# Attention values multiplied as float32, two heads in the two column halves of the array

## The chip, the cores and the metric

The kernel runs on one core of one Trainium2 chip. The metric is the device time of one execution in microseconds (us), taken as the median of the runs shown. Of the core's engines five matter here: TensorE (PE, with its weight loads shown apart as PEld), VectorE (DVE), ScalarE (ACT), GpSimd (POOL) and SyncE (SP), which issues the transfers.

## The reference, cut to what matters

The kernel computes attention and then two dense layers. The first is a mixture of eight experts whose gate is balanced by eight rounds of row and column sums, the second a layer with a squared ReLU. The change lies in the attention part, in its last product.

```python
def _attn_ref(q, k, v):                 # (4, 8, 576, 64) each: batch, heads, positions, width
    scores = scale * np.matmul(q, k.transpose(0, 1, 3, 2))
    scores = np.where(block_i >= block_j, scores, -1000000000.0)   # blocks of 64 positions
    scores = scores - np.max(scores, axis=-1, keepdims=True)
    attn = np.exp(scores)
    attn = attn / (np.sum(attn, axis=-1, keepdims=True) + 1e-09)
    return np.matmul(attn, v)           # <- the product that is changed

def _moe_ref(x, w_gate, w1, w2):        # x: 2304 x 512, eight experts of width 1024
    ...                                 # P: balanced gate
    for e in range(E):
        out += P[:, e:e + 1] * (np.maximum(x @ w1[e], 0.0) @ w2[e])

def _moe2_ref(x, w_in, w_out):          # width 2048
    r = np.maximum(x @ w_in, 0.0)
    return (r * r) @ w_out
```

## The kernel before, in words

**Pairs and steps.** The 32 heads are taken as 16 pairs. A pair has nine query blocks of 64 positions; block b sees 64(b+1) keys. The rows of both heads lie side by side in the 128 partitions, so one matmul gives the scores of one block for both heads. A pair takes R = 6 steps, and step i works on the blocks of `ROUNDS[i]`. The main loop runs over step numbers r, and in each it calls the events of `ORDER` in turn; each event serves an older step than the one before it, so several steps of a pair, and two pairs, are under way at once. The order of `ORDER` is the order in which the instructions stand on every engine.

**The events.** `S` makes the scores (tile `sc`, L547, float32). `soft` takes the maxima and applies the reciprocal sums (DVE, and POOL for the blocks of `POOL_NORM`, L592). `exp` is ACT's exponential (L579). `T` turns blocks of probabilities with 128-wide transposes into PSUM (L617). `hi` copies the turned blocks on ACT into float32r tiles (`evac_hi`, L639), and `lo` subtracts that copy from the turned block on DVE into a second float32r tile (`evac_lo`, L643). The tiles are `ptx` (group 0, from steps 0 to 2) and `pty` (group 1, from steps 3 to 5), each twice, for the high and the low part.

**The values.** `load_v` brings the values of a pair (320 KB) into tile `v`. `conv_v` splits them in the same way into one tile `vt`: the high part by DVE (L536), the low part by POOL (L537). There is one `v` and one `vt`.

**The product.** `pv(n, g, a)` (L655 to L669) makes for group g and head a the product from three float32r matmuls a part: high by high, low values by high, high by low. Group 0 has parts of 384, 256 and 128 columns, group 1 four of 192 and one of 64, so 9 and 15 matmuls. Each writes PSUM partitions 0 to 63. `PVT = (8, 9, 11, 12)` places the four calls of a pair at its steps 8, 9, 11 and 12. One step later `pv_copy` (ACT, L674) brings the result into `xs`, head a in partitions 64a to 64a+63, and after the last of them `xout` (SP, L679) sends `xs` on.

**The other work.** Once eight pairs are through and the inputs of the first third of the tokens have been split and summed (`form`, on ACT, POOL and DVE, L240 among them), `do_fill` adds work of the expert layer to each step: products `m` (L305 to L307, six float32r matmuls of 384 columns) and outputs `y` (L367 to L369, six of 512 columns), some 1.05 us of PE by the planner's own cost a step. The pieces are counted by step, not by time. What the attention loop has not done of them follows right behind it, and then the rest of the two layers, in one list in a fixed order. The loads at the start stand in the order in which the code issues them: the first pair's k and q, `v`, the identity, the gate's weights, three blocks of expert weights, and then the second pair's k and q (L523).

Of the kernel before, what the change touches and what calls it, by code (L numbers as in the profile page):

```python
# [8 lines left out]
F32 = mybir.dt.float32  # L9
F32R = mybir.dt.float32r  # L10
I32 = mybir.dt.int32
I64 = mybir.dt.int64
ACTF = mybir.ActivationFunctionType
ALU = mybir.AluOpType
# [16 lines left out]
PAIRS = NB * NH // 2  # L31
SCALE = 0.125
R = 6
# [21 lines left out]

POFF = {7: 0, 3: 2496, 6: 512, 5: 2752, 8: 1024, 0: 1600, 2: 1728, 4: 1984, 1: 2368}

ORDER = ["soft", "pvc", "load", "hi", "exp", "S", "fill", "pv", "lo", "T"]

POOL_NORM = (1, 4, 6, 8)  # L60

VSTEP = 7

LAG = 3

PVT = (8, 9, 11, 12)

PVD = 1

# [26 lines left out]
def fused_kernel(ctx: ExitStack, tc: tile.TileContext, q, k, v, wg, w1, w2, u1, u2, ident, out):  # L96
    nc = tc.nc
# [365 lines left out]
    for S in range(len(stages) + 1):  # L463
        a = products(S) if S < len(stages) else []
        b = outputs(S - 1) if S else []
        if a:
            piece(lambda S=S: begin(S))
        for z in WEAVE:
            src = a if z == "m" else b
# [28 lines left out]
    def attention():  # L498
        with ExitStack() as es:
            at = es.enter_context(tc.tile_pool(name="at", bufs=1))  # L500
            st = es.enter_context(tc.tile_pool(name="st", bufs=4))
            qkv = es.enter_context(tc.tile_pool(name="qkv", bufs=2))
            vp = es.enter_context(tc.tile_pool(name="vp", bufs=1))
            psa = es.enter_context(tc.tile_pool(name="psa", bufs=1, space=PSUM))
            ps = extra["ps"] = es.enter_context(tc.tile_pool(name="ps", bufs=4, space=PSUM))
            vt = at.tile([128, 5, 2, 128], F32R, name="vt")

            pt_x = [at.tile([128, 14, 128], F32R, name=f"ptx{z}") for z in range(2)]
            pt_y = [at.tile([128, 13, 128], F32R, name=f"pty{z}") for z in range(2)]
            scs = [psa.tile([128, w], F32, name=f"sc{z}") for z, w in enumerate((512, 512, 1024))]  # L510
            pb = at.tile([128, 3136], F32, name="pb")
            xs = at.tile([128, 9, 64], F32, name="xs")
            raws = {}
            stat = {}
            tps = {}
            pvs = {}
# [12 lines left out]
            def load_v(n):  # L529
                t = raws["v", n] = vp.tile([128, 640], F32, tag="v", name="v")  # L530
                nc.sync.dma_start(out=t, in_=v[n])

            def conv_v(n):
                t = raws.pop(("v", n)).rearrange("p (j a d) -> p j a d", a=2, d=64)
                hi = vt[:, :, :, 0:64]
                nc.vector.tensor_copy(out=hi, in_=t)  # L536
                nc.gpsimd.tensor_tensor(out=vt[:, :, :, 64:128], in0=t, in1=hi.bitcast(F32), op=ALU.subtract)  # L537

            def width(b):
                return 64 * (b + 1)  # L540
# [78 lines left out]
                    tps[5, 1] = ps.tile([128, 512], F32, tag="g", name="T5")  # L619
                    nc.tensor.transpose(tps[5, 1][0:64, 0:128], pblock(8, 4, 64), idn)  # L620

            def evac_places(i):
                tp = tps[i % 2]
                if i == 0:
                    yield tp, [t[:, 1:14:4] for t in pt_x]
                elif i == 1:
                    yield tp.rearrange("p (a b) c -> p a b c", b=2), [
                        t[:, 2:10].rearrange("p (a b) c -> p a b c", b=4)[:, :, 0:2] for t in pt_x
                    ]
                elif i == 2:  # L630
                    yield tp, [t[:, 0:13:4] for t in pt_x]
                else:
                    yield tp, [t[:, i - 3:i + 7:3] for t in pt_y]
                if i == 5:
                    yield tps[5, 1][0:64, 0:128], [t[0:64, 12] for t in pt_y]

            def evac_hi(i):
                for src, dst in evac_places(i):
                    nc.scalar.activation(out=dst[0], in_=src, func=ACTF.Copy)  # L639

            def evac_lo(i):
                for src, dst in evac_places(i):
                    nc.vector.tensor_tensor(out=dst[1], in0=src, in1=dst[0].bitcast(F32), op=ALU.subtract)  # L643

            def place(n):

# [5 lines left out]
                        t, h = divmod(9 * b + i - 2 * GT * g, 2)  # L652
                        yield g, i, num, (slice(t, t + num), kk, h)

            def pv(n, g, a):  # L655
                p = pvs[g, a] = ps.tile([128, 512], F32, tag="g", name="pv")
                ca = slice(64 * a, 64 * a + 64)
                mm = []
                pts = pt_y if g else pt_x
                if g == 0:  # L660
                    parts = [(0, 0, 6, 0), (1, 6, 4, 128), (2, 12, 2, 256)]
                else:
                    parts = [(j, 3 * j, 3, 0) for j in range(4)] + [(4, 12, 1, 128)]
                for j, i0, nbk, o0 in parts:
                    for t, z in ((0, 0), (0, 64), (1, 0)):
                        mm.append((p[0:64, o0:o0 + 64 * nbk], vt[:, j, a, z:z + 64], pts[t][:, i0:i0 + nbk, ca]))
                mm.append(mm.pop(1))
                for z, (o, l, r) in enumerate(mm):
                    nc.tensor.matmul(o, l, r, start=(z == 0), stop=(z == len(mm) - 1))  # L669

            def pv_copy(g, a):
                w, i0 = (192, 6) if g else (384, 0)
                dst = xs.rearrange("p b c -> p (b c)")[64 * a:64 * a + 64, 64 * i0:64 * i0 + w]
                nc.scalar.activation(out=dst, in_=pvs.pop((g, a))[0:64, :w], func=ACTF.Copy)  # L674

            def xout(n):
                for g, z, num, (t, kk, h) in place(n):
# [34 lines left out]
                yield from form(0)  # L712

            load_qk(0)
            load_v(0)

            for t in pt_y:
                nc.gpsimd.memset(t[64:128, 12].bitcast(F32), 0.0)
            for b in (0, 2, 4, 6):
                nc.gpsimd.memset(pb[:, POFF[b] + width(b):POFF[b] + width(b) + 64], 0.0)  # L720
            nc.sync.dma_start(out=idn, in_=ident)
# [18 lines left out]
            def at_step(fn, r):  # L740
                if 0 <= r < total:
                    fn(*divmod(r, R))
# [11 lines left out]
                     divmod(r - LAG, R) if 0 <= r - LAG < total else None)  # L754

            def turn(r):
                return [(n, z // 2, z % 2) for z, o in enumerate(PVT) for n in [(r - o) // R]
                        if (r - o) % R == 0 and 0 <= n < PAIRS]

            def do_pv(r):  # L760
# [1 line left out]
                    pv(*t)  # L762

            def do_pvc(r):
                for n, g, a in turn(r - PVD):
                    pv_copy(g, a)
                    if g == 1 and a == 1:
                        xout(n)
                        if n >= 4:
                            later.append(n)  # L770
                        if n == 7:
                            tasks.append(first_ready())

            def do_loads(r):
                n, i = divmod(r, R)
                if later:
                    logits_part(later.pop())
                if i == 0 and n + 1 < PAIRS:
                    load_qk(n + 1)
                if r >= VSTEP and (r - VSTEP) % R == 0 and (r - VSTEP) // R < PAIRS:  # L780
                    conv_v((r - VSTEP) // R)
                    if (r - VSTEP) // R + 1 < PAIRS:
                        load_v((r - VSTEP) // R + 1)

            events = {
                "S": lambda r: at_step(scores, r),
                "soft": do_soft,
                "exp": lambda r: at_step(expo, r - 1),
                "T": lambda r: at_step(trans, r - LAG - 1),
                "hi": lambda r: at_step(lambda _, j: evac_hi(j), r - LAG - 2),  # L790
                "lo": lambda r: at_step(lambda _, j: evac_lo(j), r - LAG - 2),
                "pv": do_pv, "pvc": do_pvc, "fill": do_fill, "load": do_loads,
            }
            for r in range(total + R + LAG):
                for e in ORDER:
                    events[e](r)
# [130 lines left out]
```

## Time and profile before

| | us |
|---|---|
| median of 3 runs | 2171.06 |
| lowest and highest | 2168.55 and 2171.75 |
| the profiled execution | 2169.18 |
| its span, first to last instruction | 2167.4 |
| mean granted TensorE clock of it, as a share | 0.996 |

The profile shows one execution. A matmul's duration in it is that of one matmul through the pipeline; matmuls behind each other overlap, so a group's time is read from the chain of work, where each stretch counts once. One float32 matmul stands in the trace as two matmul records with a weight load each; a float32r matmul stands as one. The attention part goes from the start to about 282 us, the rest of the span is the two layers.

### The profile page before, as it was taken

The numbers are of one execution on the slowest core, as the hardware profiler recorded it, in microseconds if no ns is written. First come the engines' busy times: TensorE is split into PE (matmuls) and PEld (weight loads), VectorE is DVE, ScalarE is ACT, GpSimd is POOL, SyncE is SP. The second block draws the span as 40 slices with busy tenths as digits, with TensorE's granted clock in tenths as the row PEclk, the third lists the DMA queues.
The fourth block names the chain that finished last, engine by engine and source line by source line (L and its number), as shares of the span: only waits on it lengthen the run. The fifth ranks groups of instructions, "written<-read, shape, count | busy, mean of one in ns | idle before, by whom it ended". The sixth has DMA issues, their size and how long they took to land.

```text
span 2167.4 us, 32907 instructions
## 1 busy us (share of the span) xinstructions
PE 2124.5 (98%) x11091; PEld 1880.0 (87%) x11091; DVE 1654.7 (76%) x3018; ACT 932.0 (43%) x2299; POOL 1601.5 (74%) x1784
## 2 busy tenths in 40 slices
PE   8989999999999999999999999999999999999998
PEld 6878888889888898889889888988888888888887
DVE  7988858778787767777877767777887667878776
ACT  6766643334434343333434353333434343343432
POOL 4356466678888778778888777787887768878874
PEclk9999999999999999999999999999999999999999
DMA  4433222232323332233232332333222222131211
GB/s 148 121 102 98 67 63 67 85 103 83 98 83 98 98 98 96 85 108 95 81 98 83 98 112 73 108 103 99 82 82 74 69 99 86 59 127 59 95 62 49
DMA packets 80713, 194.62 MB, mean 90 GB/s; under 512 B 26144, under 2 KB 27296, under 8 KB 80544
## 3 DMA queue, kind: packets, MB, share of 16 engines
q1 hardware_dynamic: 80544, 192.53, 28.3%
q8 instruction: 87, 1.43, 0.3%
q14 instruction: 82, 0.67, 0.1%
HBM read 169.95 MB, written 20.97 MB: 88 GB/s over the span
## 4 chain that ended last, share of the span: by engine, by line
PE 87%; DVE 9%; ACT 2%; issue 1%; DMA 1%; SPq 0%; POOL 0%; DVEq 0%; ACTq 0%; POOLq 0%
PE y L369 14%; PE y L368 14%; PE y L367 14%; PE m L306 12%; PE m L305 12%; PE m L307 12%; PE sc L547 3%; PE pv L669 3%; DVE c L285 2%; PE T L617 2%; DVE c L311 1%; DVE h L287 1%; ACT h L286 1%; DVE acc L380 1%; DVE mu L311 0%
## 5 line engine op out<-in xcount | busy, mean ns | idle before, releaser
L367 PE MATMUL y<-b,h 128*128 128x512 f32 x1440 | 566.2, 393 | 18.2 <-ACT h L286 17.6
L369 PE MATMUL y<-b,h 128*128 128x512 f32 x1440 | 574.3, 399 | 0.3 <-DVE h L281 0.3
L305 PE MATMUL m<-x,ah 128*128 128x384 f32 x1680 | 568.3, 338 | 2.2 <-DVE pty L643 1.3
L368 PE MATMUL y<-b,h 128*128 128x512 f32 x1440 | 568.7, 395 | 0.0
L306 PE MATMUL m<-x,ah 128*128 128x384 f32 x1680 | 565.8, 337 | 0.0
L307 PE MATMUL m<-x,al 128*128 128x384 f32 x1680 | 562.1, 335 | 0.0
L166 POOL TENSOR_TENSOR al<-sum,ah 128x256 fp32r<-128x256 f32 x480 | 392.1, 831 | 215.6 <-ACT ah L165 199.6
L280 ACT ACTIVATE h<-c 128x384 fp32r<-128x384 f32 x384 | 201.8, 526 | 736.9 <-DVE c L311 736.7
L387 DVE SCALAR_TENSOR_TENSOR acc<-y,prob,acc 128x512 f32<-128x512 f32 x516 | 383.9, 744 | 80.0 <-PE y L369 78.8
L166 POOL TENSOR_TENSOR al<-raww,ah 128x256 fp32r<-128x256 f32 x360 | 296.3, 823 | 186.2 <-ACT ah L165 141.4
L281 DVE SCALAR_TENSOR_TENSOR h<-c,h 128x384 fp32r<-128x384 f32 x384 | 275.2, 717 | 186.9 <-ACT h L280 186.4
L305 PEld LDWEIGHTS m<-x,ah 128*128 128x128 f32 x1680 | 315.9, 188 | 34.5 <-DVE pty L643 1.6
L306 PEld LDWEIGHTS m<-x,ah 128*128 128x128 f32 x1680 | 315.8, 188 | 34.0 <-issue 1.0
L174 POOL TENSOR_TENSOR b<-raww,b 128x512 fp32r<-128x512 f32 x240 | 325.0, 1354 | 16.1 <-ACT b L173 15.5
L369 PEld LDWEIGHTS y<-b,h 128*128 128x128 f32 x1440 | 269.9, 187 | 64.8 <-DVE h L287 5.9
L367 PEld LDWEIGHTS y<-b,h 128*128 128x128 f32 x1440 | 270.7, 188 | 59.8 <-ACT h L286 23.8
L307 PEld LDWEIGHTS m<-x,al 128*128 128x128 f32 x1680 | 315.6, 188 | 0.0
L368 PEld LDWEIGHTS y<-b,h 128*128 128x128 f32 x1440 | 270.2, 188 | 35.1 <-issue 0.8
L165 ACT ACTIVATE ah<-sum 128x256 fp32r<-128x256 f32 x480 | 183.4, 406 | 148.0 <-POOL sum L149 143.5
L149 POOL TENSOR_TENSOR sum<-raww 128x256 f32<-128x256 f32 x240 | 213.3, 889 | 0.0
L311 DVE TENSOR_TENSOR c<-m,u 128x384 f32<-128x384 f32 x240 | 131.9, 550 | 39.8 <-PE m L307 39.4
L173 ACT ACTIVATE b<-raww 128x512 fp32r<-128x512 f32 x240 | 148.6, 620 | 0.0
(93 smaller groups left out, 2456.9 us busy)
## 6 DMA issues: line engine op xcount, KB each, us to landing
raww<-w_t SPq DMA_DIRECT2D x192, 512.0 KB, 3.7
raww<-w1f SPq DMA_DIRECT2D x24, 512.0 KB, 3.3
raww<-w2f SPq DMA_DIRECT2D x24, 512.0 KB, 3.3
q<-q_d SPq DMA_DIRECT2D x15, 576.0 KB, 4.1
raw<-w_in_bits SPq DMA_DIRECT2D x16, 512.0 KB, 5.2
raw<-w_out_bits SPq DMA_DIRECT2D x16, 512.0 KB, 5.0
acc<-xd SPq DMA_DIRECT2D x30, 256.0 KB, 4.3
v<-v_p SPq DMA_DIRECT2D x16, 320.0 KB, 3.0
```

The costliest lines, as they stand in the source:

```text
L149: nc.gpsimd.tensor_tensor(out=t[:, o], in0=x, in1=y, op=op)
L166: nc.gpsimd.tensor_tensor(out=lo, in0=src, in1=hi.bitcast(F32), op=ALU.subtract)
L174: nc.gpsimd.tensor_tensor(out=lo[:, f], in0=src, in1=hi[:, f].bitcast(F32), op=ALU.subtract)
L280: nc.scalar.activation(out=hh, in_=x3, func=ACTF.Relu)
L281: wait.append(lambda: nc.vector.scalar_tensor_tensor(out=hl, in0=x3, scalar=0.0, in1=hh.bitcast(F32), op0=ALU.max, op1=ALU.subtract,))
L305: nc.tensor.matmul(p, ah[:, k2], bh[:, k2], start=(k2 == 0), stop=False)
L306: nc.tensor.matmul(p, ah[:, k2], bl[:, k2], start=False, stop=False)
L307: nc.tensor.matmul(p, al[:, k2], bh[:, k2], start=False, stop=(k2 == 1))
L367: nc.tensor.matmul(p, hh, bh[:, f], start=(f == 0), stop=False)
L368: nc.tensor.matmul(p, hh, bl[:, f], start=False, stop=False)
L369: nc.tensor.matmul(p, hl, bh[:, f], start=False, stop=(f == 1))
L387: nc.vector.scalar_tensor_tensor(out=a, in0=p, scalar=pe, in1=a, op0=ALU.mult, op1=ALU.add)
```

## The change

The products of the probabilities with the values take float32 operands. So neither the probabilities nor the values are split: the event `lo`, `conv_v` and the tile `vt` go, `ptx` and `pty` stand once, and the values are read from tile `v`, of which there are now two. `pv(n, g)` makes both heads of a group in one call: the matmuls of the two heads alternate, head 0 into PSUM partitions 0 to 63, head 1 into 64 to 127 of the same tile. `pv_copy` copies both heads at once. `PVT` places the two calls of a pair at steps 8 and 11. The first `load_v` moves from the start to step 1, so behind the second pair's k and q.

```diff
-ORDER = ["soft", "pvc", "load", "hi", "exp", "S", "fill", "pv", "lo", "T"]
+ORDER = ["soft", "pvc", "load", "hi", "exp", "S", "fill", "pv", "T"]
-VSTEP = 7
+VSTEP = 1
-PVT = (8, 9, 11, 12)
+PVT = (8, 11)
...
-            vp = es.enter_context(tc.tile_pool(name="vp", bufs=1))
+            vp = es.enter_context(tc.tile_pool(name="vp", bufs=2))
...
-            vt = at.tile([128, 5, 2, 128], F32R, name="vt")
-
-            pt_x = [at.tile([128, 14, 128], F32R, name=f"ptx{z}") for z in range(2)]
-            pt_y = [at.tile([128, 13, 128], F32R, name=f"pty{z}") for z in range(2)]
+
+            pt_x = at.tile([128, 14, 128], F32, name="ptx")
+            pt_y = at.tile([128, 13, 128], F32, name="pty")
...
-            def conv_v(n):
-                t = raws.pop(("v", n)).rearrange("p (j a d) -> p j a d", a=2, d=64)
-                hi = vt[:, :, :, 0:64]
-                nc.vector.tensor_copy(out=hi, in_=t)
-                nc.gpsimd.tensor_tensor(out=vt[:, :, :, 64:128], in0=t, in1=hi.bitcast(F32), op=ALU.subtract)
...
+                nc.scalar.activation(out=dst, in_=tp, func=ACTF.Copy)
...
-            def evac_lo(i):
-                for src, dst in evac_places(i):
-                    nc.vector.tensor_tensor(out=dst[1], in0=src, in1=dst[0].bitcast(F32), op=ALU.subtract)
...
-            def pv(n, g, a):
-                p = pvs[g, a] = ps.tile([128, 512], F32, tag="g", name="pv")
-                ca = slice(64 * a, 64 * a + 64)
-                mm = []
-                pts = pt_y if g else pt_x
+            def pv(n, g):
+
+                p = pvs[g] = ps.tile([128, 512], F32, tag="g", name="pv")
+                vn = raws["v", n].rearrange("p (j a d) -> p j a d", a=2, d=64)
+                pt = pt_y if g else pt_x
...
-                for j, i0, nbk, o0 in parts:
-                    for t, z in ((0, 0), (0, 64), (1, 0)):
-                        mm.append((p[0:64, o0:o0 + 64 * nbk], vt[:, j, a, z:z + 64], pts[t][:, i0:i0 + nbk, ca]))
-                mm.append(mm.pop(1))
-                for z, (o, l, r) in enumerate(mm):
-                    nc.tensor.matmul(o, l, r, start=(z == 0), stop=(z == len(mm) - 1))
-
-            def pv_copy(g, a):
+                for z, (j, i0, nbk, o0) in enumerate(parts):
+                    for a in range(2):
+                        ca = slice(64 * a, 64 * a + 64)
+                        nc.tensor.matmul(
+                            p[ca, o0:o0 + 64 * nbk], vn[:, j, a], pt[:, i0:i0 + nbk, ca],
+                            start=(z == 0), stop=(z == len(parts) - 1),
+                        )
+
+            def pv_copy(g):
                 w, i0 = (192, 6) if g else (384, 0)
-                dst = xs.rearrange("p b c -> p (b c)")[64 * a:64 * a + 64, 64 * i0:64 * i0 + w]
-                nc.scalar.activation(out=dst, in_=pvs.pop((g, a))[0:64, :w], func=ACTF.Copy)
+                dst = xs.rearrange("p b c -> p (b c)")[:, 64 * i0:64 * i0 + w]
+                nc.scalar.activation(out=dst, in_=pvs.pop(g)[:, :w], func=ACTF.Copy)
...
             load_qk(0)
-            load_v(0)
...
                 if r >= VSTEP and (r - VSTEP) % R == 0 and (r - VSTEP) // R < PAIRS:
-                    conv_v((r - VSTEP) // R)
-                    if (r - VSTEP) // R + 1 < PAIRS:
-                        load_v((r - VSTEP) // R + 1)
+                    load_v((r - VSTEP) // R)
```

On PE, in the third pair's steps 2 and 3, this stood in a row before: between two lots of scores (`sc`) the nine float32r matmuls of group 0 for one head (`ptx_109` is the high part, `ptx_110` the low one), then the transposes.

```order
L547 MATMUL sc_115<-k,q 128x320
L669 MATMUL pv<-ptx_109,vt 64x384
L669 MATMUL pv<-ptx_110,vt 64x384
L669 MATMUL pv<-ptx_109,vt 64x256 x2
L669 MATMUL pv<-ptx_110,vt 64x256
L669 MATMUL pv<-ptx_109,vt 64x128 x2
L669 MATMUL pv<-ptx_110,vt 64x128
L669 MATMUL pv<-ptx_109,vt 64x384
L617 MATMUL T<-idn,pb 128x128 x4
```

At the same place of the changed kernel stand the six float32 matmuls of both heads; of each two, the first is head 0 and the second head 1.

```order
L540 MATMUL sc_112<-k,q 128x320
L650 MATMUL pv<-ptx,v 64x384 x2
L650 MATMUL pv<-ptx,v 64x256 x2
L650 MATMUL pv<-ptx,v 64x128 x2
L610 MATMUL T<-idn,pb 128x128 x4
L540 MATMUL sc_110<-k,q 128x448
```

Both heads have moved into one place, and the second place of group 0, one step later, is gone; group 1 goes the same way.

On SP, at the start, this stood before (`w_t` are the expert weights, the last two rows the second pair's k and q):

```order
L527 DMA q<-q_d 128x384
L531 DMA v<-v_p 128x640
L721 DMA idn<-ident 128x128
L722 DMA wgt<-w_gate 128x32
L137 DMA raww_138<-w_t 128x1024
L137 DMA raww_140<-w_t 128x1024
L137 DMA raww_142<-w_t 128x1024
L523 DMA k<-k_t 128x576
L523 DMA q<-q_d 128x1152
```

And this stands there now:

```order
L526 DMA q<-q_d 128x384
L703 DMA idn<-ident 128x128
L704 DMA wgt<-w_gate 128x32
L137 DMA raww_132<-w_t 128x1024
L137 DMA raww_134<-w_t 128x1024
L137 DMA raww_136<-w_t 128x1024
L522 DMA k<-k_t 128x576
L522 DMA q<-q_d 128x1152
L530 DMA v<-v_p 128x640
```

The first pair's values have moved behind the second pair's k and q.

## Rows read from the trace of the kernel before

**Rows 1.** The page, busy time, share and instructions of the engines.

```profile
PE 2124.5 (98%) x11091; PEld 1880.0 (87%) x11091; DVE 1654.7 (76%) x3018; ACT 932.0 (43%) x2299; POOL 1601.5 (74%) x1784
```

**Rows 2.** Windows: stretch, length, each engine's busy us, clock, DMA share, GB/s.

```profile
core 0: us, PE busy (x) PEld busy (x) DVE busy (x) ACT busy (x) POOL busy (x), PEclk, DMA share, GB/s
43.93:56.30 12.37, 12.37 (x95) 10.20 (x95) 11.47 (x41) 9.93 (x29) 4.71 (x5) 1.00 0.40 124
...
204.47:223.85 19.38, 19.38 (x136) 16.83 (x135) 14.19 (x47) 13.48 (x38) 6.42 (x8) 1.00 0.26 76
...
420.00:820.00 400.00, 400.00 (x2006) 359.30 (x2006) 302.67 (x483) 160.22 (x379) 322.77 (x359) 1.00 0.30 95
```

**Rows 3.** The chain through one pair: start us, length us, what.

```profile
43.93 0.87 PE sc L547 x4
44.80 1.24 PE pv L669 x15
46.04 0.44 PE T L617 x4
...
48.44 1.14 PE pv L669 x9
...
50.77 1.04 PE pv L669 x9
...
52.36 0.86 PE sc L547 x2
...
54.63 1.24 PE pv L669 x15
```

**Rows 4.** Weight loads to 290 us: line, shape, count | busy us, mean ns | idle.

```profile
L669 PEld LDWEIGHTS pv<-pty,vt 128*64 128x64 f32 x480 | 43.6, 135 | 6.6 <-issue 1.9 <-DVE pty L643 1.1
...
L305 PEld LDWEIGHTS m<-x,ah 128*128 128x128 f32 x52 | 9.8, 188 | 5.9 <-DVE pty L643 1.6 <-DVE acc L380 1.2 <-PE sc L547 1.0
```

**Rows 5.** The other engines' lines that go or shrink, to 290 us.

```profile
L643 DVE TENSOR_TENSOR ptx<-T,ptx 128x512 fp32r<-128x512 f32 x48 | 32.8, 683 | 4.6 <-ACT ptx L639 4.6
L643 DVE TENSOR_TENSOR pty<-T,pty 128x512 fp32r<-128x512 f32 x48 | 32.8, 683 | 3.9 <-ACT pty L639 3.4
...
L537 POOL TENSOR_TENSOR vt<-v,vt 128x640 fp32r<-128x640 f32 x16 | 24.9, 1558 | 34.7 <-DVE vt L536 27.4 <-PE sc L547 4.2 <-PE lp L693 2.6
...
L674 ACT ACTIVATE xs<-pv 64x384 f32<-64x384 f32 x32 | 15.4, 481 | 10.6 <-PE pv L669 7.0 <-DMA xd<-xs 3.2 <-ACT ah L165 0.3
...
L536 DVE CAST vt<-v 128x640 fp32r<-128x640 f32 x16 | 9.2, 578 | 0.0
```

**Rows 6.** The chain at the start, and what it released.

```profile
7.82 8.78 DMA q<-q_d
...
16.74 2.05 PE sc L547 x4
```

**Rows 7.** Windows of the start and of three longer intervals between pairs.

```profile
0.00:20.00 20.00, 11.76 (x38) 8.35 (x39) 8.69 (x35) 7.82 (x22) 3.02 (x13) 0.88 0.69 232
...
30.47:43.93 13.46, 12.68 (x97) 10.37 (x96) 12.80 (x42) 11.18 (x34) 8.75 (x11) 1.00 0.37 116
...
139.46:162.63 23.17, 17.95 (x117) 14.29 (x116) 21.66 (x48) 15.97 (x45) 20.49 (x21) 0.93 0.34 112
162.63:184.59 21.96, 21.27 (x148) 18.69 (x146) 21.07 (x57) 15.68 (x45) 17.27 (x20) 1.00 0.34 98
```

**Rows 8.** The same windows for PE's work on tile m alone, with its count.

```profile
139.46:162.63 23.17, 2.73 (x12) 0.93 0.34 112
162.63:184.59 21.96, 9.66 (x42) 1.00 0.34 98
```

**Rows 9.** The chain late in the attention: a product's matmul, POOL's split, gate logits.

```profile
182.56 0.17 PE m L305
...
270.26 1.57 POOL vt L537
...
282.19 1.20 PE lp L693 x10
```

More of the change, by code (lines that the diff above doesn't have):

```diff
@@ L620, in trans, with evac @@
                     nc.tensor.transpose(tps[5, 1][0:64, 0:128], pblock(8, 4, 64), idn)
-            def evac_places(i):
+            def evac(i):
                 tp = tps[i % 2]
[L624 to L631, printed above, removed]
-                else:
-                    yield tp, [t[:, i - 3:i + 7:3] for t in pt_y]
+                if i == 1:
+                    dst = pt_x[:, 2:10].rearrange("p (a b) c -> p a b c", b=4)[:, :, 0:2]
+                    tp = tp.rearrange("p (a b) c -> p a b c", b=2)
+                elif i < 3:
+                    dst = pt_x[:, 1 - i // 2:14 - i // 2:4]
+                else:
+                    dst = pt_y[:, i - 3:i + 7:3]
+                nc.scalar.activation(out=dst, in_=tp, func=ACTF.Copy)
                 if i == 5:
-                    yield tps[5, 1][0:64, 0:128], [t[0:64, 12] for t in pt_y]
-            def evac_hi(i):
-                for src, dst in evac_places(i):
-                    nc.scalar.activation(out=dst[0], in_=src, func=ACTF.Copy)
-            def evac_lo(i):
-                for src, dst in evac_places(i):
-                    nc.vector.tensor_tensor(out=dst[1], in0=src, in1=dst[0].bitcast(F32), op=ALU.subtract)
+                    nc.scalar.activation(out=pt_y[0:64, 12], in_=tps[5, 1][0:64, 0:128], func=ACTF.Copy)
             def place(n):
@@ L714, in attention @@
             load_qk(0)
-            load_v(0)
-            for t in pt_y:
-                nc.gpsimd.memset(t[64:128, 12].bitcast(F32), 0.0)
+            nc.gpsimd.memset(pt_y[64:128, 12], 0.0)
             for b in (0, 2, 4, 6):
@@ L756, in turn @@
             def turn(r):
-                return [(n, z // 2, z % 2) for z, o in enumerate(PVT) for n in [(r - o) // R]
+                return [(n, z) for z, o in enumerate(PVT) for n in [(r - o) // R]
                         if (r - o) % R == 0 and 0 <= n < PAIRS]
@@ L764, in do_pvc @@
             def do_pvc(r):
-                for n, g, a in turn(r - PVD):
-                    pv_copy(g, a)
-                    if g == 1 and a == 1:
+                for n, g in turn(r - PVD):
+                    pv_copy(g)
+                    if g == 1:
                         xout(n)
@@ L789, in attention @@
                 "T": lambda r: at_step(trans, r - LAG - 1),
-                "hi": lambda r: at_step(lambda _, j: evac_hi(j), r - LAG - 2),
-                "lo": lambda r: at_step(lambda _, j: evac_lo(j), r - LAG - 2),
+                "hi": lambda r: at_step(lambda _, j: evac(j), r - LAG - 2),
                 "pv": do_pv, "pvc": do_pvc, "fill": do_fill, "load": do_loads,
```

## The prediction, as it was put on record

> **What bounds the kernel now.** I read the page first: PE is busy 98% of the span, no other engine over 76% [rows 1]. A busy PE in this view is not yet a full one, so the next view is the chain of waits in order of time, and there the reader is to see that through a whole pair every piece is PE's, one behind the other [rows 3]. A pair's interval there is 12.37 us, and DVE is busy 11.47 and ACT 9.93 of it [rows 2]. So PE sets the pace and DVE is close behind. In the later intervals the planner's pieces are added on PE (19.38 us an interval, PE busy throughout, DVE 14.19) and the two layers after the attention are PE's from end to end [rows 2]. The pieces are counted by step and the list is fixed, so work that the attention saves moves the end of the attention and with it the end of the kernel, one to one. The change touches nothing behind that.
>
> Three stretches of the attention are not PE's. At the start PE waits for the second pair's q, which takes 8.78 us to land while the expert weights come in as well [rows 6]. The third pair's interval is 13.46 us against 12.37 [rows 2, 7]. And while the first expert inputs are formed, two intervals take 23.17 and 21.96 us, with DVE busy 21.66 and 21.07 of them [rows 7].
>
> **PE's products.** Before, a pair costs 1.24 twice for group 1 and 1.14 and 1.04 for group 0 [rows 3], 4.66 us in all, 24 x 2 matmuls of float32r. Each head has 768 columns in group 0 and 832 in group 1.
>
> A float32 column's price is in the scores: the lot of 512 columns takes 0.86 us [rows 3], 1.68 ns a column. In group 0 three float32r columns cost 1.04/768 = 1.35 ns. So for one head alone float32 is dearer: 1600 x 1.68 = 2.69 us a head, 5.38 us for both if they go one behind the other. That is the upper end, 0.72 us a pair more than now. The lower end is both heads wholly beside each other, 2.69 us, 1.97 less than now.
>
> The trace of before has no place where matmuls of different column halves follow each other (every product sits in partitions 0 to 63, and the scores use all columns), so no row shows which end holds. I take the side by side end, less its lead. What speaks for it: the operands name separate halves of the columns, separate weights, separate output partitions, and the weight loads show that the kernel's products are laid on half the columns (128*64 in [rows 4]). The starts keep the program's order, and a head's own two passes of a part can't overlap. So the pass order is high of head 0, low of head 0 beside high of head 1, low of head 1 beside the next part's high of head 0, and so on: one pass of the first part stands alone. In group 0 that is 768 x 1.68 = 1.29 and a lead of 384 x 0.84 = 0.32, in group 1 832 x 1.68 = 1.40 and 192 x 0.84 = 0.16. Together 3.17 us, and with 0.1 us more, by which the two equal products of group 0 already differ (1.14 and 1.04 [rows 3]), 3.27. Gain 4.66 - 3.27 = 1.39 us a pair, 16 pairs: **22.2 us**. The ends are 31.5 gained and 11.5 lost.
>
> [...]
>
> **Weight loads.** There were 48 a pair and are 32 (16 float32 matmuls, two each). In group 1 each of the 15 matmuls takes 1.24/15 = 83 ns [rows 3], though its weight load lasts 135 [rows 4]: the loads run under the matmuls before them. I cost them at nothing; the cover is the matmul in flight. If it went, one load would show between 53 ns (188 less 135, the price of 64 more columns [rows 4]) and its whole 135 ns: 32 x 16 of them, 27 to 69 us.
>
> **The other engines.** DVE loses six subtractions of about 0.683 us and a cast of 0.578 a pair [rows 5], 4.7 us or more; of 11.47 some 6.8 us stay. POOL loses 1.56 us a pair. ACT loses half of its copies of `pv`, 0.48 us of group 0 and less of group 1 [rows 5]; its 9.93 become some 9.1 us. A pair's interval in the plain part is forecast at 12.37 - 1.39 = 11.0, so all three stay under PE; ACT, the new second, is the closest. A float32 copy on ACT costs what the float32r one did (same elements). The last product of a pair stands at step 11 instead of 12, so `xs` is sent on a step earlier; its copies wait for PE anyway.
>
> **The start.** The first values, 320 KB, no longer stand ahead of the second pair's q. At the 232 GB/s of the first 20 us [rows 7] that is 0.328 MB / 232 = 1.4 us, and PE waits for exactly that transfer [rows 6]. Gain **1.4 us** (0 to 1.5). The values land behind q instead; they are wanted seven steps later. Later loads of values stand behind a pair's k and q on SP, which wait there for the scores of the pair before the last; the values are needed seven steps after that, and with two tiles `v` the load waits for a product two steps back. PE's products now wait for that transfer directly, with the pair's later scores queued behind; I cost it at nothing for those seven steps.
>
> **Stalls that lose their cause.** What the long intervals hold beyond PE's work: the third pair's 13.46 - 12.37 = 1.1. The first long one has the pair's 12.37, 12 matmuls of `m` [rows 8] at 0.173 (0.17 in [rows 9]) = 2.1, and gate logits of 1.2 [rows 9], so 15.7 of 23.17: 7.5 us of stall. The second has 42 matmuls, 7.3, and the same rest, 20.9 of 21.96: 1.1. In the last pairs PE waits for POOL's split of the values, 1.57 us on the chain [rows 9]. DVE loses some 5 us in each long interval. But in the first POOL is busy 20.49 us [rows 7] and loses only 1.56, so that interval can't fall below some 19 us: of 4.2 us at most, 1.4 is the product's gain, and I take 2.5. With 0.8, 0.7 and 1.0 for the other three, **5 us** (0 to 10).
>
> **Sum.** 22.2 + 1.4 + 5.0 = 28.6 us. The profiled execution took 2169.18, so 2140.6; the median of the runs, 2171.06, lies 1.9 above it, so 2142.5. I say **2142**, between them and nearer to the median.
>
> **The rivals.** First, *the halves don't run beside each other*: float32 passes go one by one. Then PE loses 11.5 us, the start still gains 1.4, and the stalls give some 4 (less, since PE is later): 2171.06 + 6.1 = 2177 (2174 to 2182). This is the slower side. It decides from 5.0 us a pair for the products on (4.66 plus 5.4/16), so it needs most of the columns one behind the other. For it: no row shows an overlap. Against it: no row shows a shared part that is full.
>
> Second, *the weight loads come into the open*, since with two heads in turn a load for one half must pass the other half's running matmul. At 53 ns each that is 27 us, which eats the gain of the overlap: 2142 + 27 = 2169, no change; without overlap it is 2204. [...] The trace speaks against it as far as it goes, since 83 ns matmuls over 135 ns loads on the same rows are all of [rows 3, 4]; loads of alternating halves it doesn't show.
>
> Third, *ACT or the chain of steps takes over* in the plain intervals: steps without products fall to some 1.3 us of PE (0.87 of scores and 0.44 of transposes [rows 3]), and ACT at 9.1 of 11.0 us has little slack in them. Up to 0.6 us in eight intervals, 5 us: 2147. It lies within the forecast's own spread.
>
> **How the numbers follow.** Forecast with its third-rival spread 0.75; loads in the open with overlap 0.06; no overlap 0.15; both 0.04. The forecast's own ends are 31.5 + 1.5 + 10 gained, 2128, and some 17 gained, 2154. For 8 in 10 the range must reach over the second rival's 2169: 2128 to 2170. A measurement of this kernel can tell about 0.2%, 4.3 us, from no change: faster means below 2166.7, slower above 2175.4. Faster 0.76, the same 0.09 (second rival and the lower part of the first), slower 0.15.
>
> **What would show it.** In the profile after: the products (12 matmul records in group 0, 20 in group 1) should take some 1.6 us each on the chain, and intervals between pairs 11.0 in the plain part; starts of the two heads' matmuls should lie closer together than one pass lasts. If group 1 takes 2.8 us, the halves don't overlap; if single matmuls wait with PEld as the releaser, the loads are open. The first scores of the second pair should start at some 15.3 us instead of 16.74. DVE should fall under 7 us an interval. I am wrong if the plain intervals are 12 us or more, or if ACT ends the waits there.

## The result, and the profile after

The changed kernel takes 2143.7 us (median of four runs, 2142.88 to 2144.25), beside 2170.29 us for the kernel before on the same chip: ratio 0.9877, 95% interval 0.986 to 0.9895. That is 26.6 us gained, where 28.6 were forecast. The prediction of 2142 holds. But its step on how the two heads' products start doesn't, nor does the step that nothing behind the attention is touched. For the first, a lead was counted that isn't there, and a cost of about the same size wasn't counted, so the sum came out. The rest of this document is about that.

The profiled execution took 2144.16 us, its span is 2142.4, 25.0 shorter than the span before. PE stays at 98% [rows 1]:

```profile
PE 2105.8 (98%) x10835; PEld 1845.3 (86%) x10835; DVE 1590.9 (74%) x2890; ACT 916.2 (43%) x2267; POOL 1575.3 (74%) x1767
```

The chain through one pair, to be read against [rows 3] (start us, length us, what). Every piece is PE's, as before, and a pair's interval is 50.07 - 39.05 = 11.02 us:

```profile
39.05 0.87 PE sc L540 x4
39.92 0.44 PE T L610 x4
...
42.31 1.45 PE pv L650 x12
43.76 0.59 PE T L610 x4
...
45.65 0.86 PE sc L540 x2
46.51 0.44 PE T L610 x4
...
47.92 1.56 PE pv L650 x20
49.48 0.59 PE T L610 x4
50.07 0.87 PE sc L540 x4
```

The two products take 1.45 + 1.56 = 3.01 us a pair where four took 4.66. The four transposes right behind a product take 0.59 us instead of the 0.44 of the pair's others. That is 0.15 twice a pair, and a pair keeps 4.66 - 3.01 - 0.30 = 1.35 us of gain.

The windows of a plain interval and of the two that follow pair 9 (pairs are counted from 0 from here on), where the first expert inputs are formed (columns: stretch, length, busy us of each engine, granted clock, DMA share, GB/s), against [rows 2, 7]:

```profile
38.88:49.91 11.03, 11.03 (x80) 7.85 (x79) 7.79 (x32) 9.01 (x27) 3.20 (x4) 1.00 0.48 138
107.62:129.45 21.83, 20.79 (x138) 16.94 (x137) 10.94 (x35) 12.35 (x38) 9.34 (x11) 0.84 0.25 75
129.45:148.90 19.45, 17.30 (x107) 13.20 (x106) 16.08 (x40) 14.79 (x42) 16.82 (x18) 0.91 0.29 95
```

In the plain interval DVE is at 7.79 of 11.03 and ACT at 9.01, so PE alone sets the pace. The interval of 21.83 stands where before there was one of 139.46 - 120.30 = 19.16: here the changed kernel loses 2.7 us, with the granted clock at 0.84 on average.

**Where the time went**, by the first scores of each interval in the two traces (before, after):

| stretch | before, us | after, us | gained |
|---|---|---|---|
| to the second pair's (pair 1's) scores | 16.74 | 14.82 | 1.9 |
| the next eight intervals | 103.56 | 92.80 | 10.8 (8 x 1.35) |
| the interval from pair 9 to 10 | 19.16 | 21.83 | -2.7 |
| from there to the last product (281.9; 255.0) | 142.4 | 125.6 | 16.9 |
| first layer's work behind the attention | | | 27.2 ahead |
| behind 1846 us, in the second layer | | | 25.0 ahead |

### The profile page after: what moved, and what is told of

Read it like the earlier page. It is cut to its first block, busy times and chain, and to the rows that moved or that the text cites. A ratio compares the mean times of both kernels' runs of the same rounds, so it can differ in the third digit from the quotient of the medians.

```text
span 2142.4 us, 32197 instructions
## 1 busy us (share of the span) xinstructions
PE 2105.8 (98%) x10835; PEld 1845.3 (86%) x10835; DVE 1590.9 (74%) x2890; ACT 916.2 (43%) x2267; POOL 1575.3 (74%) x1767
## 4 chain that ended last, share of the span: by engine, by line
PE 88%; DVE 8%; ACT 2%; issue 1%; POOL 0%; DMA 0%; SPq 0%; DVEq 0%; POOLq 0%; ACTq 0%
PE y L369 14%; PE y L368 14%; PE y L367 14%; PE m L306 12%; PE m L307 12%; PE m L305 12%; PE sc L540 3%; PE pv L650 2%; PE T L610 2%; DVE c L285 2%; DVE h L287 2%; DVE c L311 1%; ACT h L286 1%; DVE acc L380 1%; DVE mu L311 0%
```

## The experiments

All were compared with the kernel before on the same chip; each "ratio" is to that, with its 95% interval. Its medians there were 2169.65 us (for one half, heads apart, the subtractions kept and the relief alone), 2170.47 (both products in one step, values ahead, logits on every other step, no normalising on POOL) and 2170.98 (blocks of two parts, 128 columns, a quarter of the logits, three edits together). In the code cuts, `...` marks what is left out.

**One half for both heads.** Does the gain come from the overlap of the halves? Each head gets a tile `pv` of its own, and both use partitions 0 to 63:

```diff
...
-                            p[ca, o0:o0 + 64 * nbk], vn[:, j, a], pt[:, i0:i0 + nbk, ca],
+                            p[a][0:64, o0:o0 + 64 * nbk], vn[:, j, a], pt[:, i0:i0 + nbk, ca],
...
```

> The changed kernel, but both heads of a group write partitions 0 to 63, each its own PSUM tile, so all products sit in the same half of the columns; the copies are again one a head. Everything else is as changed. Theory (the gain is that the two halves run beside each other): a pair's products take 1600 x 2 x 1.68 ns = 5.4 us instead of some 3.3, plain intervals 11.0 + 2.1 = 13.1 us, the whole some 2143.7 + 16 x 2.1 = 2177 us, slower than before. Rival (the gain comes from VectorE's removed work and the start): within 5 us of 2144.

Measured: 2184.18 us, ratio 1.0062 (1.0047 to 1.0077). Its chain:

```profile
56.14 2.98 PE pv L650 x20
59.12 0.59 PE T L610 x4
...
62.97 2.74 PE pv L650 x12
65.71 0.59 PE T L610 x4
```

The products take 5.72 us instead of 3.01, the interval is 13.72. So without the overlap the change is a loss, and the overlap is worth 40 us. It came out 7 us above the 2177 that was expected, since a pair's products take 0.34 more than the 5.38 that was reckoned, and the transposes behind them 0.59 here too, 0.30 more a pair. So that cost isn't one of two halves taking turns.

**Heads one behind the other.** If starts keep the program's order, a product of all of head 0 and then all of head 1 can't overlap:

```diff
-                for z, (j, i0, nbk, o0) in enumerate(parts):
-                    for a in range(2):
+                for a in range(2):
+                    for z, (j, i0, nbk, o0) in enumerate(parts):
...
```

> The changed kernel with all parts of head 0 first and then all parts of head 1, in their two halves as before this edit. Theory (matmuls start in the program's order, so only neighbours can run beside each other): they overlap at the seam alone, 5.1 to 5.4 us a pair, 2172 to 2177 us. Rival (the engine takes the second half's matmuls as soon as that half is free, whatever stands between): 2144 us as with the heads in turn.

Measured: 2169.36 us, ratio 0.9994 (0.9984 to 1.0003), between the two that were expected. Its chain:

```profile
58.39 2.14 PE pv L650 x11
60.53 0.59 PE T L610 x4
...
64.69 2.59 PE pv L650 x19
67.28 0.59 PE T L610 x4
```

4.73 us a pair, neither 3.01 nor 5.72. With the 0.30 of the transposes that is 5.03 us and no change, which fits the 5.0 that the prediction gives as the limit for its first rival. The single records of the first product tell why. Head 0's six passes (a float32 matmul has two, a record each) start at 58.316, 58.690, 59.012, 59.228, 59.444 and 59.553; head 1's first starts at 59.018, beside head 0's third, with three matmuls that stand ahead of it in the program still to start. In the second product, too, head 1's first pass starts (65.646) with three of head 0's still to start. So in both products a matmul for the free half started ahead of the program's order, but not from any distance: three matmuls early and no more.

**Heads in blocks of two parts.** The distance put to a test: two parts (four records) of a head, then two of the other.

```diff
-                for z, (j, i0, nbk, o0) in enumerate(parts):
-                    for a in range(2):
+                for y in range(0, len(parts), 2):
+                    for a, z in [(a, z) for a in range(2) for z in range(y, min(y + 2, len(parts)))]:
+                        j, i0, nbk, o0 = parts[z]
...
```

> The changed kernel with the heads in blocks of two parts (two float32 matmuls, four records) instead of part by part. If a matmul for the free half may start up to three matmuls ahead of the program's order, as the heads one behind the other showed, head 1's first record of a block starts beside head 0's first or second and the products stay at 3.0 to 3.2 us a pair: 2143 to 2147 us. If only the very next matmul can go ahead, head 1 starts beside head 0's last record of a block, two to three records late in each of five blocks: some 0.8 to 1.2 us a pair more, 2157 to 2163.

Measured: 2145.78 us, ratio 0.9886 (0.9871 to 0.99).

```profile
53.70 1.45 PE pv L651 x12
...
59.30 1.62 PE pv L651 x18
```

3.07 us a pair. In group 1 head 0's first record starts at 59.234 and head 1's at 59.248, with three of head 0's four still to start. So three matmuls early is reached here too.

**Both heads' values as weights of 128 columns.** What are the 0.15 us behind each product? Here no product uses half of the columns:

```diff
...
-                            p[ca, o0:o0 + 64 * nbk], vn[:, j, a], pt[:, i0:i0 + nbk, ca],
+                            p[a][:, o0:o0 + 64 * nbk], vn[:, j].rearrange("p a d -> p (a d)"), pt[:, i0:i0 + nbk, ca],
...
```

> The changed kernel with both heads' values as weights of all 128 columns, each head's product into a tile of its own, of which the copy takes the head's half. The heads can't overlap. If the edges of 0.3 us a product belong to float32 matmuls on half of the columns, they are gone: transposes behind a product take 0.44 instead of 0.59, the products 1600 x 1.68 x 2 = 5.38 us a pair, the plain interval 13.1 and the time 16 x 0.6 below the run with one half (2184), 2174 to 2176. If they belong to float32 products whatever their columns, the interval is 13.7 and the time 2184.

Measured, in a single execution: 2174.83 us.

```profile
52.51 2.99 PE pv L650 x20
55.50 0.44 PE T L610 x4
...
59.21 2.60 PE pv L650 x12
61.81 0.44 PE T L610 x4
```

The transposes are back at 0.44, and in the single records the passes follow each other without a gap at either end of a product. The run lies 9.3 us under the one with one half (16 x 0.6 = 9.6 expected); the interval is 13.31 against 13.72, since the records of group 1's last part, 64 columns, mostly follow each other after 0.11 us now instead of 0.055. So the extra time at the two ends of a product, from here on its edges, belongs to float32 products on half of the columns. (The 0.11 us transposes of line 613, also 64 columns of weights, show no edges; why, no run here tells.)

**Both products in one step.** If the edges are paid once a stretch and not once a product, two products back to back pay half (the rest of the edit chooses between the two tiles `ptx`):

```diff
-PVT = (8, 11)
+PVT = (11, 11)
...
-            pt_x = at.tile([128, 14, 128], F32, name="ptx")
+            pt_xs = [at.tile([128, 14, 128], F32, name=f"ptx{z}") for z in range(2)]
...
```

> The changed kernel with both groups' products of a pair in one step, directly behind each other; the tile ptx stands twice for that. TensorE's instructions are the same. Theory (each stretch of products costs some 0.3 us at its edges: 0.10 ahead of its first matmul, 0.05 in its second pass, 0.10 and 0.06 at the transposes behind it): one pair of edges a pair less, the plain interval 10.7 us, the whole 2139 us. Rival 1 (the cost belongs to each group, not to the change between the products and other work): 11.0 us, 2144 us. Rival 2 (five steps of 1.3 us of TensorE follow each other and ScalarE, some 1.5 us a step, sets the pace): waits on ScalarE appear and the interval is 11.0 or more although the edges are gone.

Measured: 2143.19 us, ratio 0.9872 (0.9858 to 0.9887): not to be told from the changed kernel; 2139 was expected.

```profile
58.96 2.86 PE pv L651 x32
61.82 0.59 PE T L610 x4
...
67.42 1.10 PE sc L540 x2
```

The edges are paid once: 2.86 us instead of 3.01 and one row of 0.59, so 0.30 us less a pair. But the scores of 512 columns, 0.86 before, now take 1.10, and the weight load ahead of them waited for ACT:

```profile
PEld sc L540 <- ACT pb L572: 0.2, 1, 0.2
```

(columns: engine and line waited for, us, times, longest; from 66 to 69 us). Of 0.30 us, 0.24 go into this new wait. The interval is 10.97.

**The subtractions kept.** How much of the gain is DVE's? The `lo` tiles and the split of the values, which is DVE's and POOL's, are made as before, but nothing reads them:

```diff
-ORDER = ["soft", "pvc", "load", "hi", "exp", "S", "fill", "pv", "T"]
+ORDER = ["soft", "pvc", "load", "hi", "exp", "S", "fill", "pv", "lo", "T"]
...
```

> The changed kernel, with VectorE's subtractions of the turned blocks and its cast of the values, and GpSimd's split of the values, put back into tiles that nobody reads. TensorE's work is as changed. Theory (VectorE's relief pays only in the stalls, 5 us in the sum): VectorE would be busy some 11.4 us of a plain interval of 11.0, so it now sets the interval at 11.5 to 12 us there and the stalls come back: 2152 to 2160 us. Rival (the relief is worth nothing): 2144 us.

Measured: 2157.17 us, ratio 0.994 (0.9925 to 0.9955). A plain interval:

```profile
54.24:65.71 11.47, 11.35 (x80) 7.71 (x79) 11.40 (x41) 8.90 (x28) 4.37 (x5) 1.00 0.46 134
```

DVE is busy 11.40 of 11.47 us, and the chain there goes from one DVE piece to the next; the four intervals behind it are 11.96 to 12.72, where the changed kernel's are 11.61 to 11.69. The largest single loss, 4.2 us, is in the interval from pair 10 to 11 (23.67 instead of 19.45). So the relief is worth 13.5 us once the products are short. The clock may have a part in that: up to 380 us this trace shows 34 us at half clock, that of the changed kernel 17.

**The relief alone.** The kernel before without DVE's subtractions. The third product of each part multiplies the high part of the probabilities once more, so PE's work is the same and the low part is left out of the sum; the split of the values stays:

```diff
-ORDER = ["soft", "pvc", "load", "hi", "exp", "S", "fill", "pv", "lo", "T"]
+ORDER = ["soft", "pvc", "load", "hi", "exp", "S", "fill", "pv", "T"]
...
-                        mm.append((p[0:64, o0:o0 + 64 * nbk], vt[:, j, a, z:z + 64], pts[t][:, i0:i0 + nbk, ca]))
+                        mm.append((p[0:64, o0:o0 + 64 * nbk], vt[:, j, a, z:z + 64], pts[0][:, i0:i0 + nbk, ca]))
...
```

> The kernel before, without VectorE's subtractions of the turned blocks; the third product of each part multiplies the high part of the probabilities once more, so the low part is left out of the sum. TensorE's work is as before, float32r. Theory (VectorE's relief alone is worth the stalls, of 9.7 us in the three long intervals some 5): 2164 to 2167 us. Rival (it is worth nothing without TensorE's shorter products): 2170 us. The products themselves keep 4.66 us a pair and the plain intervals 12.4 us by both.

Measured: 2167.76 us, ratio 0.9991 (0.9982 to 1.0001).

```profile
54.63:66.93 12.30, 12.30 (x96) 10.27 (x94) 7.88 (x33) 9.71 (x30) 4.67 (x6) 1.00 0.42 124
```

DVE fell from 11.47 to 7.88 and the interval from 12.37 to 12.30. With PE's products unchanged the relief brings some 2 us, which the interval of the ratio doesn't tell from nothing. In its trace the interval from pair 9 to 10 is 2.3 us longer than before (21.49), with the granted clock at 0.5 there from 130.2 to 137.0 us, which may hide a part. The two halves of the change bring more together than apart: the relief 2, the shorter products without it 12.5, both together 26.6.

**Values ahead of q again.** The start's term by itself:

```diff
...
+            load_v(0)
...
-                if r >= VSTEP and (r - VSTEP) % R == 0 and (r - VSTEP) // R < PAIRS:
+                if r > VSTEP and (r - VSTEP) % R == 0 and (r - VSTEP) // R < PAIRS:
...
```

> The changed kernel with the first pair's values loaded at the start again, ahead of the second pair's q, as before. Nothing else differs. Theory (the 320 KB ahead of q cost 1.4 us): the second pair's first scores start at some 16.3 us instead of 14.8, and the whole is 1.4 us longer, 2145 us. Rival (the landing of q varies by as much from one execution to the next; with the new order it has shown 14.8, 15.0, 15.9 and 16.6 us, with the old one 16.3 and 16.7): a start anywhere from 15 to 17 us, and a whole that can't be told from 2143.7.

Measured: 2144.39 us, ratio 0.9881 (0.9866 to 0.9896); the time doesn't tell. In its trace the second pair's scores start at 16.02. Over all traces of this study they start between 14.82 and 16.63 with the values behind q (eleven runs, median 15.0) and at 16.02, 16.33 and 16.74 with the values ahead (three runs). By the medians the order is worth some 1.3 us, but the spread from run to run is nearly 2 and the two ranges overlap.

**Gate logits on every other step.** The interval that became longer holds the gate logits of the first expert tiles, 48 matmuls of 8 columns. In both kernels the first 16 stand apart and the other 32 behind each other. Before, a product stood between the 16 and the 32; in the changed kernel only scores and transposes do. The chain there, and the windows:

```profile
109.93 1.69 PE lg L784 x16
...
112.87 5.08 PE lg L784 x32
117.94 2.76 PE pv L650 x12
120.70 0.89 PE T L610 x4
```

```profile
112.00:116.00 4.00, 4.00 (x29) 3.84 (x28) 1.97 (x5) 1.64 (x6) 2.50 (x4) 0.81 0.26 101
116.00:120.00 4.00, 4.00 (x18) 2.86 (x19) 0.00 (x0) 0.18 (x1) 0.85 (x1) 0.50 0.00 0
```

The granted clock goes to 0.50 within the lot of 32 (from 114.45 to 121.28 us). The lot takes 5.08 us; in the trace of before the same 32 matmuls took 3.47 at full clock (1.00). The product after it takes 2.76 us instead of 1.45, the transposes 0.89 instead of 0.59: 3.2 us more in all. Does the clock stay full with a product between the lots? Spreading them:

```diff
...
-                yield from logits(ps, "g")
+                for _ in logits(ps, "g"):
+                    yield
+                    yield
...
```

> The changed kernel with the three lots of gate logits (lg, 16 narrow matmul records each) one a step instead of two in one step, so that the first product of a pair stands between the second and the third lot, as a product did before the change. The inputs of the first experts are formed one step later. [...]

Measured: 2143.38 us, ratio 0.9871 (0.9855 to 0.9888): no gain over the changed kernel's 2143.7 that can be told. The clock fell all the same (0.64 and 0.51 from 112 to 120 us); the last product ended 2 us earlier, but the first layer's work is only 0.5 us further ahead: the layers' pieces are taken along later there (the first `y` at 168.0 us instead of 164.6), and what the attention doesn't take is left for behind it.

**A quarter of the gate logits.** Are the lots the cause? Only the first of four parts of each logit is computed, the other 36 matmuls are left out:

```diff
...
-                for kk in range(KD):
+                for kk in range(1):
...
-                        start=(kk == 0), stop=(kk == KD - 1),
+                        start=True, stop=True,
...
```

> The changed kernel with a quarter of the gate logits' matmuls behind pair 9 (kk 0 alone, 12 of 48; the rest is left out). If the lots of matmuls of 8 columns bring the clock down, the granted clock stays full from 105 to 130 us, and attention ends up to 7 us earlier than in the changed kernel (36 x 0.105 = 3.8 us of matmuls and the 3.2 lost to the clock), less what the forming of the first inputs holds back: 2137 to 2142. If the clock falls there for another reason, a stretch at half the clock is still seen between 105 and 130 us, and only the 3.8 us go.

Measured, in a single execution: 2134.9 us, below the 2137 to 2142 expected. Its chain and windows:

```profile
110.03 0.34 PE lg L784 x4
...
111.63 0.79 PE lg L784 x8
112.42 1.45 PE pv L650 x12
113.87 0.60 PE T L610 x4
```

```profile
110.00:115.00 5.00, 5.00 (x39) 3.77 (x38) 3.87 (x13) 3.70 (x15) 3.62 (x5) 1.00 0.67 229
115.00:120.00 5.00, 5.00 (x40) 3.72 (x39) 3.66 (x13) 4.47 (x15) 3.90 (x5) 1.00 0.16 39
```

The clock stays full here and the layer's work comes 7.1 us earlier than in the changed kernel to the end of the attention (9.4 at the end of the kernel). The matmuls left out are 36 x 0.105 = 3.8; the other 3.3 agree with the 3.2 that the chain shows for the clock. So where the clock falls there, it costs some 3 us. That the lots are the cause is likely and not shown: one trace with a quarter of them has no fall beside them, of the thirteen with all 48 eleven have one, and two have none (the kernel before, and the three edits together). It isn't a cost of this change alone: it was seen in the run of the relief alone too, whose products are placed as in the kernel before (granted clock 0.5 from 130.2 to 137.0 us).

**No normalising on POOL.** `POOL_NORM = ()` instead of `(1, 4, 6, 8)`: DVE, now with room, normalises all tiles.

> The changed kernel with all probability blocks scaled by VectorE, none by GpSimd; VectorE now has the room. Theory (where the expert inputs are formed GpSimd, busy 21.8 of 24.5 us there, is what TensorE's transposes wait for, 7.5 us by PE and PEld): GpSimd loses some 3.2 us an interval, VectorE gains some 2, 9.8 of 11.0 us in the plain part, the whole 2139 to 2142 us. Rival (VectorE becomes late in the plain intervals): they grow over 11.1 us and the whole is over 2144 us.

Measured: 2142.52 us, ratio 0.9873 (0.9858 to 0.9888). The wait of PE for POOL's `pb` (one of 2.1 us from 38 to 140 us in the changed kernel) is gone, the plain interval is unchanged. The difference of 1.2 us is below what the measurement can tell.

**Three edits together** (both products in one step, no normalising on POOL, logits on every other step).

> Three small edits at once: no normalising on POOL, both products of a pair in one step with two tiles ptx, the gate logits on every other step. If each keeps what it showed alone against the changed kernel's 2143.7 (1.2, 0.5 and 0.3 us), 2141.7; if they take the same waits away, 2142.5 to 2143.5; if ACT's wait for the scores grows without POOL's share, 2143.5 to 2146.

Measured: 2139.42 us (2137.61 to 2140.3), ratio 0.9855 (0.9838 to 0.9871).

```profile
50.03:60.75 10.72, 10.72 (x79) 7.95 (x78) 7.84 (x36) 8.75 (x27) 0.00 (x0) 1.00 0.45 143
107.29:124.39 17.10, 17.10 (x137) 14.44 (x136) 9.35 (x38) 11.43 (x35) 3.06 (x3) 1.00 0.35 100
```

In its chain:

```profile
55.20 0.86 PE sc L540 x2
```

This is better than the 2141.7 of the sum of the parts. The plain interval is 10.72, the full 0.30 us under 11.02: the wait for ACT has gone and those scores take 0.86 again. Of the three edits only the one on POOL's normalising can have done that, since the run with both products in one step has the second, and the third doesn't act there. The clock stayed full beside the gate logits in the profiled run. Against the changed kernel it is 4.3 us better by the medians; the two ratios' intervals overlap, so that this is likely rather than shown.

## Why the prediction was right, and where not

**The products: right sum, wrong step.** Forecast 3.27 us a pair, measured 3.01 and 0.30 more in the transposes behind them, 3.31; 16 x 1.35 = 21.6 us where 22.2 were forecast. The agreement is luck. The step that failed is the lead of one pass ("The starts keep the program's order", and "one pass of the first part stands alone"), 0.48 us a pair. There is no lead. In the first product of a pair (chain from 53.34) the passes of the two heads start at 53.267 and 53.274, 53.641 and 53.647, 53.963 and 53.970: high beside high and low beside low, 7 ns apart. The timeline shows the first pair of passes (start, us together, engine, line, shapes, count):

```profile
53.27 0.54 PE L650 MATMUL pv<-ptx,v 128*64 128x384 f32 x2
```

So the whole 1600 x 1.68 = 2.69 us of the lower end is reached. In the trace of before the nine matmuls of group 0 do start in the program's order (48.034 to 49.237 us), but there every product is on the same half. The runs with the heads apart and in blocks show why it is otherwise here: a matmul for the free half started three matmuls early there (59.018 and 59.248 us), and one suffices here.

What stood in the lead's place were the edges, which the working didn't have. The first weight load of a product starts here with its matmul at 53.27 us, 0.36 behind the start of the last scores' matmul (52.91). In the kernel before it starts under the scores, at 48.01 like their last matmul; here it doesn't:

```profile
53.27 0.20 PEld L650 LDWEIGHTS pv<-ptx,v 128*64 128x64 f32 x4 [0.44 <-ACT pb L572]
```

The first pass is 0.09 us late, the second 0.05, the first transpose behind the product 0.09 and the second 0.06: 0.29 us a product by the single records, 0.6 a pair, against the 0.48 + 0.1 of lead and margin. The two errors cancel within 0.04 us a pair. With both heads in one half they don't: there the working is off by 7 us.

The float32r products of the kernel before, on half of the columns too, show no such edges: behind group 0's last matmul of 384 columns the first transpose starts after 0.176 us and another such matmul after 0.177, and behind group 1 it is 0.03 late. What in these float32 products makes the edges, no run here tells.

**Weight loads: right.** They cost nothing inside a product: the passes of 192 columns follow each other after 0.156 to 0.163 us, which is the price of the columns alone (192 x 0.84 ns = 0.161 us), though a load lasts 0.136 and uses all 128 rows, as the matmul it runs under does. The rival of loads in the open is ruled out; only a product's first load no longer starts with the last scores' matmul (53.27 us against 52.91, above).

**No overlap: a real alternative, mis-sized.** The run with one half gives what this rival described, at 2184 instead of 2177: the edges again, which the working lacks, 16 x 0.6 = 9.6 us.

**The other engines.** ACT was forecast at 9.1 and is at 9.01; its copies of 128x512 take 0.595 (`ptx`) and 0.599 us (`pty`) on average as float32, where they took 0.594 and 0.596 as float32r. DVE was to fall under 7 and is at 7.79: the sums of [rows 5] would give 6.8, but one of a pair's three `nm` instructions of two columns (line 564) now shows 0.99 us, where the other two and all three of before show 0.16 to 0.17:

```profile
53.01 0.99 DVE L564 TENSOR_SCALAR nm<-mx 128x2 f32<-128x2 f32 x1
```

Why, no run here tells. It has no effect on the time, with PE at 11.02.

**The start: right** as far as its spread lets one say: 1.9 us in this pair of traces, 1.3 by the medians of all, 1.4 forecast. The chain there still waits for `q`:

```profile
7.37 7.32 DMA q<-q_d
...
14.82 1.43 PE sc L540 x4
```

**The stalls: 5 forecast, 3.7 measured** (27.2 less 21.6 and 1.9). The sum hides two larger pieces. From pair 10 on the intervals give back 7.4 us more than their products (16.9 less 7 x 1.35). The first of them, the prediction's first long one, gives 2.4 of that, as forecast (2.5); the next, for which 0.7 was forecast, gives nothing; the largest piece, 3.6, is in the last stretch (from 36.9 to 30.6 us), in which POOL's split of the values no longer stands. Against that, the interval from pair 9 to 10 loses 2.7 where its products should have gained 1.35. Of these 4.0 us the clock beside the gate logits accounts for some 3.2 (3.2 by the chain, 3.3 by the run with fewer logits); the rest isn't settled. The prediction nowhere took the clock for something that the change could move.

**Behind the attention: "The change touches nothing behind that", but 1.8 us were lost there.** Behind a wait of PE for ACT of 1.9 us (to 1846.7 us) the clock is at half from 1848.4 us on, for 3.4 us. The kernel before has the same wait (1.94 us, to 1838.3 us), and its clock stays full. The windows of the changed kernel and, below, of the run with both products in one step, where the same instructions ran:

```profile
1846.00:1852.00 6.00, 5.31 (x17) 4.40 (x18) 5.38 (x8) 4.10 (x10) 5.84 (x6) 0.72 0.22 80
```

```profile
1846.00:1852.00 6.00, 5.04 (x23) 4.16 (x24) 5.38 (x8) 4.11 (x10) 5.84 (x6) 1.00 0.27 87
```

That run keeps its whole lead to the end (26.6 us at 360 us and at 2110 us). Such a stretch of 3.4 us starts between 1804 and 1873 us in seven of the fourteen traces (the changed kernel's, heads apart, blocks of two, values ahead, logits spread, few logits, no normalising on POOL; in two of them twice) and in the others, the kernel before among them, not. No run tells what decides it.

## What to carry to other kernels

If a product fills only half of the array's columns, try two independent ones in alternation: here they ran wholly beside each other (3.01 us a pair where one half alone took 5.72), float32 passes and weight loads included, as long as they stood within three matmuls of each other in the program (3.07 in blocks of two parts, but 4.73 with one head behind the other). Each stretch of half-column float32 matmuls among full ones cost some 0.3 us at its ends here, so put such stretches together, but look at which buffer that makes someone wait for: in this kernel the wait took most of it back. And take the second engine down with the first: the relief was worth some 2 us with PE at its old length, and 13.5 us with PE short.

## What the runs showed of the hardware that was not expected

- Matmuls of the two column halves started 6 to 7 ns apart, not a pass apart, and with the heads apart a matmul started (59.018 us) ahead of three earlier ones of the program, all for the other half (59.228 us and later).
- Float32 matmuls with 64 columns of weights cost 0.29 us at the ends of a stretch with two halves; the transposes behind them show it with one half alike (0.59 us), with 128 columns of weights not (0.44). Float32r matmuls with 64 columns show 0.03 us or less.
- The granted clock went to 0.50 within and behind lots of matmuls of 8 columns, with PE busy without a break (4.00 of 4.00 us in both rows from 112 to 120 us, clock 0.81 and 0.50). Why it didn't fall in the trace of before, nor with the three edits together, while it did with the lots merely spread, is open.
